# Output projection weights loaded as one 36,864-byte run per partition, and the attention output projected in one piece at the end

## The chip, the core and the metric

The kernel runs on one core of a Trainium2 chip. The core has a matrix engine (TensorE, PE in the profile), VectorE (DVE), ScalarE (ACT), GpSimd (POOL) and SyncE (SP). SP and ACT issue transfers to 16 DMA engines that the core's queues share. On-chip data lies in SBUF and in the accumulators' memory PSUM, both with 128 partitions. The metric is device time in microseconds for one execution; lower is better.

## The reference

One decode step (one token) for a batch of 4, with an attention block and a small MLP side by side on the same normalised input. Cut to what matters:

```python
xn = layernorm(A_x)                                   # [4, 1, 576]
# attention: 32 query heads, 16 key/value heads, the last W = 2048 positions of 8192
q  = (xn @ wq) as [4, 32, 1, 128]
s  = einsum("bhqd,bhkd->bhqk", q, k[:, :, -2048:]) * 128 ** -0.5
o  = einsum("bhqk,bhkd->bhqd", softmax(s), v[:, :, -2048:])
A  = o as [4, 1, 4096] @ wo                           # wo: [4096, 576]
# MLP: 576 -> 576 (gelu) -> 576, residual x1, 576 -> 4608 (gelu) -> 576
B  = x1 + gelu(layernorm(x1) @ w3) @ w4               # w4: [4608, 576]
out = A_x + A + B                                     # bf16, [4, 1, 576]
```

Everything is bf16 outside the accumulators. The caches that are read take 2 x 16 x 2 MB, wo 4.7 MB, wq 4.7 MB, w3 and w4 5.3 MB each.

## The kernel before

Instructions are recorded with a key by `add` and `add_dma`, sorted by key on each engine, and written out engine by engine, each with its semaphore waits (lines 163 to 176 and 543 to 603). An engine's own order is therefore fixed; the engines meet through semaphores. The two long stages are hardware loops of four iterations, one for the keys and one for the values.

**Transfers.** All loads but the 4-row input come from SP's queue, in this order: wq, w1, w2, w3, keys of the 16 key/value heads (2 MB each, ring `kring` of four slots), values (2 MB each, ring `vring` of four slots), with wo behind the fourth value load, and four pieces of w4 at the end (`W4P`: row tiles 0 to 14, 14 to 28, 28 to 34, 34 to 36 of 36). A key or value load puts 128 runs of 16,384 bytes on 128 partitions; its source is walked as 32 blocks of positions by 4 batches. Value load g waits until the product with the values of head g - 4 has been read (`PV{g-4}`), so value load 4 waits for `PV0`. wo waits for `T119`, since it overwrites the key ring. It is read as `(h p r) n -> p h (r n)`: partition p gets, for each of 8 groups of 512 rows, 4 neighbouring rows (4,608 bytes), which makes 1,024 runs. w4 piece n waits for the last value product that uses its part of `vring` (`PV12`, `PV13`, `PV14`, `PV14`).

**Keys.** PE transposes each 128x128 block of keys (line 332), DVE and ACT copy the result to SBUF (lines 339, 340), PE multiplies it with the queries (line 348). Softmax over all heads follows at once (lines 374 to 409).

**Values.** For each of the 16 heads g, `pe_PV` (line 416) runs 64 matmuls of 8 columns, and DVE multiplies the result by the reciprocal sums into eight columns of `OTn` (line 424). `OTn` is [128 features, 128 (head, batch) columns].

**Output projection.** `AO_CH` cuts the 16 heads in two chunks. `pe_sel` (line 434) brings `OTn`'s rows into wo's row order by 16 matmuls with columns of the identity, DVE copies that to `ORT` (line 458), and `pe_AO` (line 441, by `acc_mm`) multiplies with wo. Chunk 0 (48 matmuls) stands inside the value loop under a condition on the third iteration, behind `PV11`; chunk 1 (16 matmuls) stands behind the loop. The matmuls have 4 columns of weights and 288 moving columns. The 576 outputs are two halves in two 32-column tiles of the PE array, `ACC[0]` at partition 0 in PSUM bank 0 and `ACC[1]` at partition 32 in bank 1. The same two accumulators take x + x1 (`pe_t1`) and all of w4's products (`MO0`, `MO1`, `MO2`, and for the last piece `MOl0` and `MOl1`, one for each half). Two copies to SBUF (lines 539, 540) and two 4-row stores, from SP and from ACT, end the program.

Of the kernel before, what the change touches and what calls it, by code (L numbers as in the profile page):

```python
# [5 lines left out]
FP32 = mybir.dt.float32  # L6
BF16 = mybir.dt.bfloat16
ACTF = mybir.ActivationFunctionType
# [9 lines left out]
NIT = 4  # L18
ACT_EVAC = (1, 4, 7)
WO_AFTER = 3  # L20
V0_AFTER = 8
AO_CH = ((0, 6), (6, 8))
W4P = ((0, 14), (14, 28), (28, 34), (34, 36))


# [13 lines left out]
def bass_parallel_sum__sliding_block_cached__mixer_s_mlp__decode_kernel(  # L39
# [22 lines left out]
    with ExitStack() as ctx:  # L62
        def sb(name, shape, dt):
            return ctx.enter_context(nc.sbuf_tensor(name, shape, dt))
# [13 lines left out]
        w3rag = regB_t[:, 4 * F:W3E]  # L78
        wqmain = vring_t[:, 0:4 * Hq * Dh].rearrange("p (r n) -> p r n", r=4)
        wqrag = vring_t[:, 4 * Hq * Dh:4 * Hq * Dh + Hq * Dh // 2]  # L80
        wo_sb = kring_t[:, 0:Hq * D].rearrange("p (h r n) -> p h r n", h=8, r=4)
        _o = 4 * Hq * Dh + Hq * Dh // 2
        w1main = vring_t[:, _o:_o + 4 * D].rearrange("p (r n) -> p r n", r=4)
        _o += 4 * D
# [43 lines left out]
        PTs = sb("PTs", [128, NT, 32], BF16)  # L128
        PTg = sb("PTg", [128, NPG, NT, B, 2], BF16)
        OTn = sb("OTn", [128, 128], BF16)  # L130
        ORT = sb("ORT", [128, 4, 8, B], BF16)
        t1 = sb("t1", [B, D], FP32)
        out_t = sb("out_sb", [32 + B, HALF], BF16)
        out_sb = [out_t[32 * h:32 * h + B, :] for h in range(2)]

        ps = ctx.enter_context(nc.psum_tensor("ps", [128, 8, 512], FP32))[:]
        Sps = ps[:, 0:4, :]
        tb = [ps[:, 4 + k, :].bitcast(BF16).rearrange("p (t d) -> p t d", t=8) for k in range(NTB)]
        ACC = [ps[32 * k:32 * k + B, k, 0:HALF] for k in range(2)]
        ORps = ps[:, 2, 0:128].rearrange("p (r h b) -> p r h b", r=4, h=8)  # L140
        rinvps = ps[:, 3, 0:128]
        OTps = lambda g: ps[:, 4 + g % 4, 0:8]
        Qps = ps[:, 0:2, :]
# [19 lines left out]
        def add(engine, emit, waits=(), sig=None, key=0.0, loop=None):  # L163
            seqc[0] += 1
            prog[engine].append(Op(emit, waits, sig, key, seqc[0], loop))

        def add_dma(pairs, skey, waits=(), key=0.0, engine="sp"):
            if skey not in S:
                S[skey] = sem("s_" + "_".join(str(k) for k in (skey if isinstance(skey, tuple) else (skey,))))
            dma_count[skey] = dma_count.get(skey, 0) + 16 * len(pairs)  # L170

            def emit(e):
                for o_, i_ in pairs:
                    e.dma_start(o_, i_).then_inc(S[skey], 16)  # L174
            add(engine, emit, waits, None, key)
            return ("dma", skey, dma_count[skey])
# [57 lines left out]
        for g in range(G):  # L234
            kk = KS + g if g else V0_AFTER + 0.5
            w = [f"PV{g - NVS}"] if g >= NVS else (["hs1"] if g < WQ_SLOTS else [])
            ev_v.append(add_dma(kv_pairs(vring_t, g % NVS, A_v_cache, g), ("v", g % NVS), w, kk))
            if g == WO_AFTER:
                ev_wo = add_dma([(wo_sb.rearrange("p h r n -> p h (r n)"), A_wo.rearrange("(h p r) n -> p h (r n)", h=8, r=4))],
                                "wo", [wo_wait], kk + 0.1)  # L240
        w4_src = B_w4.rearrange("(p r) n -> p r n", r=RT)
        w4_sb = vring_t[:, 0:RT * D].rearrange("p (t n) -> p t n", n=D)
# [177 lines left out]
        for g in range(G):  # L420
            m = g % 4
            add("pe", pe_PV(g), waits=[("L", ("v", m), 16), ("L", ("pg", m), 1), ("L", ("on", m), 1)], sig=f"PV{g}", key=KV + g,
                loop=("v", g // 4))
            add("dve", lambda e, g=g: e.tensor_tensor(out=OTn[:, 8 * g:8 * g + 8], in0=OTps(g), in1=rinvB[:, 8 * g:8 * g + 8], op=ALU.mult),  # L424
                waits=["rinvB", f"PV{g}"], sig=("on", m), key=KV + g + 0.5)


        def pe_sel(a, z):
            def f(e):
                ov = OTn[:].rearrange("p (h q b e) -> p h q b e", h=8, q=2, b=B)  # L430
                ins = None
                for r in range(4):
                    for hh in range(4):
                        ins = e.matmul(ORps[32 * hh:32 * hh + 32, r, a:z, :], lhsT=ident_bf[:, r:128:4],
                                       rhs=ov[:, a:z, hh // 2, :, hh % 2], start=True, stop=True,
                                       tile_position=(0, 32 * hh), skip_group_check=True)
                return ins
            return f

        def acc_mm(e, h, lhsT, rhs, start=False, stop=False):  # L440
            return e.matmul(ACC[h], lhsT=lhsT, rhs=rhs, start=start, stop=stop, tile_position=(0, 32 * h))  # L441

        def pe_AO(a, z):
            def f(e):
                ins = None
                for hg in range(a, z):
                    for r in range(4):
                        for h in range(2):
                            ins = acc_mm(e, h, ORT[:, r, hg, :], wo_sb[:, hg, r, HALF * h:HALF * (h + 1)])
                return ins  # L450
            return f
        for n, (a, z) in enumerate(AO_CH):
            last = z == 8
            kk = KV + (20 if last else 2 * z - 0.4)
            lp = None if last else ("v", NIT - 2, "only")
            add("pe", pe_sel(a, z), waits=[("c", ("on", (2 * z - 1) % 4), (2 * z - 1) // 4 + 2)] + ([f"ORT{n - 1}"] if n else []),
                sig=f"sel{n}", key=kk, loop=lp)
            add("dve", lambda e, a=a, z=z: e.tensor_copy(out=ORT[:, :, a:z, :], in_=ORps[:, :, a:z, :]),  # L458
                waits=[f"sel{n}"], sig=f"ORT{n}", key=kk)
            add("pe", pe_AO(a, z), waits=[f"ORT{n}"] + ([ev_wo] if n == 0 else []), sig=f"AO{n}", key=kk + 0.1, loop=lp)  # L460

        def pe_t1(e):
            ins = None
# [59 lines left out]
        add("act", gelu2, waits=["h2_4"], sig="gelu2", key=KW + 0.1)  # L523
        add("dve", lambda e: e.transpose(h2T_sb[:].rearrange("p c i -> p (c i)"), PTb[:, 0:N2]), waits=["gelu2"], sig="h2T", key=KW + 0.2)  # L524

        last_p = len(W4P) - 1
        for n, (t0, t1_) in enumerate(W4P):
            def f(e, t0=t0, t1_=t1_, hs=(0, 1)):
                ins = None
                for t in range(t0, t1_):  # L530
                    for h in hs:
                        ins = acc_mm(e, h, h2T_sb[:, t, 0:B], w4_sb[:, t, HALF * h:HALF * (h + 1)], stop=(t == RT - 1))
                return ins
            if n < last_p:
                add("pe", f, waits=[ev_w4[n], "h2T"], sig=f"MO{n}", key=KT + 20 + n)
            else:
                for h in range(2):
                    add("pe", lambda e, f=f, h=h: f(e, hs=(h,)), waits=[ev_w4[n], "h2T"], sig=f"MOl{h}", key=KT + 20 + n + 0.1 * h)
# [21 lines left out]
        def emit_op(eng_name, engine, op, waited, it=None):  # L560
            for w in op.waits:
                if w[0] == "L":
                    engine.wait_ge(S[w[1]], it * w[2] + w[2] if w[2] > 1 else it + 1)
                    continue
                s_, v_ = resolve(w)
                if waited.get(s_.num, 0) >= v_:
                    continue
                if it is None:
                    waited[s_.num] = v_
                engine.wait_ge(s_, v_)  # L570
            ins = op.emit(engine)
            if op.sig is not None:
                ins.then_inc(S[eng_name] if isinstance(op.sig, str) else S[op.sig], 1)

        def emit_program(eng_name, engine):
            waited = {}
            ops = prog[eng_name]
            k = 0
            while k < len(ops):
                op = ops[k]  # L580
                if op.loop is None:
                    emit_op(eng_name, engine, op, waited)
                    k += 1
                    continue
                name = op.loop[0]
                z = k
                while z < len(ops) and ops[z].loop is not None and ops[z].loop[0] == name:
                    z += 1
                group, k = ops[k:z], z
                shapes = [[o for o in group if o.loop[1] == it and len(o.loop) == 2] for it in range(NIT)]  # L590
                assert all([o.waits for o in sh] == [o.waits for o in shapes[0]] for sh in shapes)
                only = [o for o in group if len(o.loop) == 3]
                assert group[-2 * len(shapes[0]) - len(only):][len(shapes[0]):][:len(only)] == only
                with engine.Fori(0, NIT) as it:
                    for o in shapes[0]:
                        emit_op(eng_name, engine, o, waited, it)
                    if only:
                        with engine.If(it == only[0].loop[1]):
                            for o in only:
                                emit_op(eng_name, engine, o, waited, it)  # L600

        for name, eng in (("sp", nc.sync), ("pool", nc.gpsimd), ("dve", nc.vector), ("act", nc.scalar), ("pe", nc.tensor)):
            emit_program(name, eng)
# [28 lines left out]
```

## Time and profile before

| | |
|---|---|
| median of 3 runs | 215.7 us (215.67 to 217.24) |
| the profiled execution's own time | 215.64 us |
| its span, first to last instruction | 214.4 us |
| bytes moved | 88.63 MB, 413 GB/s over the span |
| busy: PE, weight loads, DVE, ACT, POOL | 67%, 51%, 39%, 28%, 5% |
| granted TensorE clock, mean | 0.785 of full |

Times in the views are microseconds from the span's start. A row of the groups gives the line, engine and operation, the tile written and the tile read, the count, then busy time and mean length of one, then the idle time of the engine before them and what ended it. A row of the timeline gives start, length, engine and line. A row of the stages gives the stretch, then busy time and count for PE, PE's weight loads, DVE, ACT and POOL, then the granted clock, the mean busy share of the 16 DMA engines, and the rate. The chain of waits goes back from the last instruction to what released it.

### The profile page before, as it was taken

The page shows a single profiled execution, that of the slowest core. Times are in us where ns is not written, and L with a number is a line of the kernel's source. Part 1 is how long each engine was busy: PE and PEld are TensorE (multiplying, and loading weights), DVE is VectorE, ACT ScalarE, POOL GpSimd, SP SyncE. Part 2 cuts the span into 40 slices and gives each one's busy share as a digit, 9 for nine tenths or more (in the row PEclk, how much of TensorE's full clock was granted, in tenths as well). Part 3 has the DMA queues.
Part 4 walks back from the last instruction along what each step waited for, and adds up shares of the span by engine and source line. Part 5 has one row for each costly group of instructions (what it writes and reads, how often), then busy time and mean ns, then how long its engine had stood idle before and what let it go on. Part 6 is the DMA issues. An engine that isn't in the chain of part 4 may idle for free.

```text
span 214.4 us, 5735 instructions
## 1 busy us (share of the span) xinstructions
PE 143.2 (67%) x2646; PEld 109.1 (51%) x2648; DVE 84.5 (39%) x162; ACT 59.1 (28%) x71; POOL 10.0 (5%) x34
## 2 busy tenths in 40 slices
PE   0368375999999993999999719813343443973655
PEld 0115223777788883788877604813343443463523
DVE  5502603666666663466666479411111112100000
ACT  2000302566555553365666653000000000000000
POOL 8101000000010000000000000000000000000000
PEclk9999755999999999699999985555555555585589
DMA  6999999999999999999999999999999999999992
GB/s 245 434 395 439 440 410 437 428 408 431 428 431 422 431 428 434 422 434 423 431 425 431 428 407 411 424 427 431 419 434 431 431 419 434 428 434 421 424 412 113
DMA packets 7697, 88.63 MB, mean 413 GB/s; under 512 B 764, under 2 KB 1032, under 8 KB 2824
## 3 DMA queue, kind: packets, MB, share of 16 engines
q1 hardware_dynamic: 7672, 88.50, 97.8%
q8 instruction: 7, 0.11, 0.2%
q14 instruction: 2, 0.02, 0.0%
q10 hardware_dynamic: 16, 0.01, 0.0%
HBM read 88.49 MB, written 0.00 MB: 413 GB/s over the span
## 4 chain that ended last, share of the span: by engine, by line
DMA 53%; PE 36%; DVE 4%; SPq 4%; issue 2%; ACT 0%
DMA vring<-in_A_v_cache_dram 25%; PE ps L332 23%; DMA kring<-in_A_k_cache_dram 21%; PE ps L348 7%; DMA vring<-in_B_w_dram 7%; PE ps L416 5%; SPq L174 4%; DVE PTb L382 1%; DVE rmax L374 1%; DVE regB L340 1%; PE ps L441 1%; DVE PTs L390 1%; PE ps L405 0%; ACT P_sb L379 0%; DVE out_sb L539 0%
## 5 line engine op out<-in xcount | busy, mean ns | idle before, releaser
L340 DVE COPY regB<-ps 128x1024 bf16<-128x1024 bf16 x80 | 52.3, 687 | 34.7 <-PE ps L332 32.9
L332 PEld LDWEIGHTS ps<-perm_k,kring 128*128 128x128 bf16 x1024 | 58.7, 99 | 12.6 <-issue 8.7
L332 PE MATMUL ps<-perm_k,kring 128*128 128x128 bf16 x1024 | 62.1, 222 | 4.2 <-DMA kring<-in_A_k_cache_dram 4.2
L339 ACT ACTIVATE regB<-ps 128x1024 bf16<-128x1024 bf16 x48 | 47.7, 1023 | 41.4 <-PE ps L332 41.4
L416 PE MATMUL ps<-PTg,vring 128*128 128x8 bf16 x1024 | 29.2, 168 | 33.3 <-DMA vring<-in_A_v_cache_dram 31.4
L416 PEld LDWEIGHTS ps<-PTg,vring 128*128 128x128 bf16 x1024 | 28.1, 103 | 34.5 <-DMA vring<-in_A_v_cache_dram 24.3
L424 DVE TENSOR_TENSOR OTn<-ps,rinvB 128x8 bf16<-128x8 f32 x16 | 2.7, 167 | 57.3 <-PE ps L416 57.2
L540 ACT ACTIVATE out_sb<-ps 4x288 bf16<-4x288 f32 x1 | 0.4, 402 | 81.2 <-PE ps L441 81.2
L348 PE MATMUL ps<-regB,Qs 128*32 128x512 bf16 x272 | 18.7, 395 | 4.6 <-issue 3.5
L348 PEld LDWEIGHTS ps<-regB,Qs 128*32 128x32 bf16 x272 | 6.6, 97 | 10.8 <-issue 6.2
L393 DVE TENSOR_TENSOR PTg<-PTs,bmask 128x512 bf16<-128x512 bf16 x16 | 10.7, 682 | 0.0
L370 POOL COPY Qs<-Qpad 128x128 bf16<-128x128 bf16 x16 | 4.6, 296 | 93.5 <-PE ps L348 81.4
L441 PE MATMUL ps<-kring,ORT 128*4 128x288 bf16 x64 | 7.7, 431 | 0.7 <-DVE ORT L458 0.7
L441 PE MATMUL ps<-vring,h2T_sb 128*4 128x288 bf16 x72 | 5.3, 299 | 2.8 <-DMA vring<-in_B_w_dram 2.8
L511 PE MATMUL ps<-regB,x1nT 128*32 128x432 bf16 (+1 forms) x60 | 5.4, 522 | 2.1 <-DMA regB<-in_B_w_dram 1.6
L274 PE MATMUL ps<-ident_bf,xn_bf 4*128 4x4 bf16 x8 | 0.5, 169 | 8.8 <-DVE ragsrc L267 8.8
L296 PE MATMUL ps<-vring,xnT 128*32 128x512 bf16 x40 | 4.6, 629 | 1.8 <-DMA vring<-in_A_wq_dram 1.8
L441 PEld LDWEIGHTS ps<-kring,ORT 128*4 128x4 bf16 x64 | 3.8, 121 | 3.9 <-DVE ORT L458 0.9
L441 PEld LDWEIGHTS ps<-vring,h2T_sb 128*4 128x4 bf16 x72 | 3.0, 87 | 5.3 <-DMA vring<-in_B_w_dram 4.0
L383 PE MATMUL ps<-PTb,perm_p 128*128 128x512 bf16 x3 | 1.8, 608 | 4.9 <-DVE PTb L382 4.8
L274 PEld LDWEIGHTS ps<-ident_bf,xn_bf 4*128 4x128 bf16 x8 | 0.4, 112 | 8.8 <-POOL ones_f L210 6.3
L524 DVE STREAM_TRANSPOSE h2T_sb<-PTb 128x1152 bf16<-128x1152 bf16 x1 | 1.4, 1378 | 8.4 <-ACT PTb L521 8.4
(88 smaller groups left out, 61.7 us busy)
## 6 DMA issues: line engine op xcount, KB each, us to landing
kring<-in_A_k_cache_dram SPq DMA_DIRECT2D x16, 2048.0 KB, 16.1
vring<-in_A_v_cache_dram SPq DMA_DIRECT2D x16, 2048.0 KB, 17.6
regB<-in_B_w_dram SPq DMA_DIRECT2D x2, 2304.0 KB, 21.3
kring<-in_A_wo_dram SPq DMA_DIRECT2D x1, 4608.0 KB, 24.1
vring<-in_A_wq_dram SPq DMA_DIRECT2D x2, 2048.0 KB, 9.5
vring<-in_B_w_dram SPq DMA_DIRECT2D x2, 2016.0 KB, 15.7
vring<-in_B_w_dram SPq DMA_DIRECT2D x2, 576.0 KB, 13.8
vring<-in_B_w_dram SPq DMA_DIRECT2D x1, 864.0 KB, 14.7
```

The costliest lines, as they stand in the source:

```text
L174: e.dma_start(o_, i_).then_inc(S[skey], 16)
L296: ins = e.matmul(Qps[32 * j:32 * j + 32, k, :], lhsT=x_, rhs=w, start=(r == 0), stop=(r == 4), tile_position=(0, 32 * j))
L332: ins = e.transpose(tb[n % NTB][:, t, :], kring[:, g % NKS, 8 * k + t, :], perm_k[:])
L339: return "act", lambda e: e.activation(out=ktbuf[:, n % NKT], in_=src, func=ACTF.Copy)
L340: return "dve", lambda e: e.tensor_copy(out=ktbuf[:, n % NKT], in_=src)
L348: ins = e.matmul(Sps[32 * b:32 * b + 32, c4, :].rearrange("p (t i) -> p t i", t=16), lhsT=Qs[:, g % 4, b, :], rhs=kttile[:, t0:t0 + 16, b, :],
L370: P(lambda e, g=g: e.tensor_copy(out=Qs[:, g % 4], in_=Qpad[:, g]), waits=(["qT"] if g == 0 else []) + ([f"SC{g - 4}"] if g >= 3 else []), ...
L393: add("dve", lambda e, g=g: e.tensor_tensor(out=PTg[:, g % NPG], in0=PTs[:, :, 2 * g:2 * g + 2].unsqueeze(2).to_broadcast([128, NT, B, 2]) ...
L416: ins = e.matmul(OTps(g), lhsT=vring[:, g % NVS, t, :], rhs=PTg[:, g % NPG, t].rearrange("p b e -> p (b e)"), start=(t == 0), stop=(t == N ...
L424: add("dve", lambda e, g=g: e.tensor_tensor(out=OTn[:, 8 * g:8 * g + 8], in0=OTps(g), in1=rinvB[:, 8 * g:8 * g + 8], op=ALU.mult), waits=[ ...
L441: return e.matmul(ACC[h], lhsT=lhsT, rhs=rhs, start=start, stop=stop, tile_position=(0, 32 * h))
L511: ins = e.matmul(H2ps[k][32 * j:32 * j + 32, :], lhsT=x_, rhs=w, start=(r == 0), stop=(r == 4), tile_position=(0, 32 * j))
```

## The change

Three things are done together.

wo is loaded as `(h q r) n -> q h (r n)` with 4 values of q, 32 heads h and 32 rows r: partition 32q + h gets one run of 32 neighbouring rows of head h, 36,864 bytes, which makes 128 runs. The source is walked with q outermost (4), then h (32).

The attention output is no longer brought into order by PE. DVE writes each head's result to strided columns of `OTn` (batch outermost), and once all 16 heads are done one DVE transpose of 32x32 blocks turns `OTn` into `ORT`. The condition in the value loop is gone, and all 64 matmuls with wo stand behind the loop.

These 64 matmuls, and those of w4's first piece (`FOLD` = 14 row tiles), go to four 32-column tiles in place of two. `ACC[2]` and `ACC[3]` lie at partitions 64 and 96 of PSUM bank 2. Behind `MO0` ACT copies both to SBUF as fp32 (`foldc`), and two fp32 matmuls with the identity add them to `ACC[0]` and `ACC[1]` (`fold`), ahead of `MO1`.

```diff
-AO_CH = ((0, 6), (6, 8))
+FOLD = 14
...
-        wo_sb = kring_t[:, 0:Hq * D].rearrange("p (h r n) -> p h r n", h=8, r=4)
+        wo_sb = kring_t[:, 0:32 * D].rearrange("p (r n) -> p r n", r=32)
...
+        fold_sb = P_sb[:, 0:2 * HALF].bitcast(FP32)
...
-        ACC = [ps[32 * k:32 * k + B, k, 0:HALF] for k in range(2)]
-        ORps = ps[:, 2, 0:128].rearrange("p (r h b) -> p r h b", r=4, h=8)
+        ACC = [ps[32 * k:32 * k + B, min(k, 2), 0:HALF] for k in range(4)]
...
-                ev_wo = add_dma([(wo_sb.rearrange("p h r n -> p h (r n)"), A_wo.rearrange("(h p r) n -> p h (r n)", h=8, r=4))],
+                ev_wo = add_dma([(kring_t[:, 0:32 * D], A_wo.rearrange("(h q r) n -> q h (r n)", q=4, r=32))],
...
-            add("dve", lambda e, g=g: e.tensor_tensor(out=OTn[:, 8 * g:8 * g + 8], in0=OTps(g), in1=rinvB[:, 8 * g:8 * g + 8], op=ALU.mult),
+            add("dve", lambda e, g=g: e.tensor_tensor(
+                out=OTn[:].rearrange("p (b g e) -> p g b e", b=B, e=2)[:, g], in0=OTps(g).rearrange("p (b e) -> p b e", b=B),
+                in1=rinvB[:, 8 * g:8 * g + 8].rearrange("p (b e) -> p b e", b=B), op=ALU.mult),
...
-        def pe_sel(a, z):
...
+        def acc_mm(e, h, lhsT, rhs, start=False, stop=False, k0=0):
+            return e.matmul(ACC[h], lhsT=lhsT, rhs=rhs, start=start, stop=stop, tile_position=(k0, 32 * h))
+
+        def pe_AO(e):
+            ins = None
+            for r in range(32):
+                for h in range(2):
+                    ins = acc_mm(e, 2 * (r % 2) + h, ORT[:, r:128:32], wo_sb[:, r, HALF * h:HALF * (h + 1)], start=(r == 1))
+            return ins
+        add("dve", lambda e: e.transpose(ORT[:], OTn[:]), waits=[("c", ("on", m), NIT + 1) for m in range(4)], sig="ORT", key=KV + 20)
+        add("pe", pe_AO, waits=["ORT", ev_wo], sig="AO", key=KV + 20)
...
+        def pe_fold(e):
+            ins = None
+            for h in range(2):
+                k0 = 64 + 32 * h
+                ins = acc_mm(e, h, ident_f[k0:k0 + B, k0:k0 + B], fold_sb[k0:k0 + B, :], k0=k0)
+            return ins
...
+        add("act", lambda e: e.activation(out=fold_sb[64:96 + B, :], in_=ps[64:96 + B, 2, 0:HALF], func=ACTF.Copy),
+            waits=[f"MO{n_fold}"], sig="foldc", key=KT + 20 + n_fold + 0.5)
+        add("pe", pe_fold, waits=["foldc"], sig="fold", key=KT + 20 + n_fold + 0.5)
...
-                        ins = acc_mm(e, h, h2T_sb[:, t, 0:B], w4_sb[:, t, HALF * h:HALF * (h + 1)], stop=(t == RT - 1))
+                        a = 2 * (t % 2) + h if t < FOLD else h
+                        ins = acc_mm(e, a, h2T_sb[:, t, 0:B], w4_sb[:, t, HALF * h:HALF * (h + 1)], stop=(t == RT - 1 or (t == FOLD - 1 and a > 1)))
```

PE's own order from the value loop to the end, before (row L416 is one pass through the loop's body, `ps` are accumulators in PSUM, `kring` holds wo by then and `vring` w4):

```order
L416 MATMUL ps<-PTg,vring 128x8 x256
L598 COMPARE_AND_BRANCH
L434 MATMUL ps<-OTn,ident_bf 32x24 x16
L441 MATMUL ps<-kring,ORT 4x288 x48
L598 UNCONDITIONAL_BRANCH
L594 REGISTER_ALU
L594 COMPARE_AND_BRANCH
L434 MATMUL ps<-OTn,ident_bf 32x8 x16
L441 MATMUL ps<-kring,ORT 4x288 x16
L441 MATMUL ps<-vring,h2T_sb 4x288 x72
```

The same place on PE with the change, where `P_sb` holds the two accumulators that are folded in:

```order
L416 MATMUL ps<-PTg,vring 128x8 x256
L584 REGISTER_ALU
L584 COMPARE_AND_BRANCH
L431 MATMUL ps<-kring,ORT 4x288 x64
L431 MATMUL ps<-vring,h2T_sb 4x288 x28
L431 MATMUL ps<-P_sb,ident_f 4x288 x2
L431 MATMUL ps<-vring,h2T_sb 4x288 x44
```

The 48 matmuls with wo have moved from inside the loop to behind it, the 32 matmuls of `pe_sel` are gone, and the fold stands between the first 28 and the other 44 matmuls with w4.

SP's queue around the load of wo, as a difference (the sizes are those of the destination; `kring` is wo's place):

```order
 L174 DMA kring<-in_A_k_cache_dram 128x1x8192 x7
 L174 DMA vring<-in_A_v_cache_dram 128x1x8192 x3
-L174 DMA kring<-in_A_wo_dram 128x8x2304
+L174 DMA kring<-in_A_wo_dram 128x1x18432
 L174 DMA vring<-in_A_v_cache_dram 128x1x8192 x12
 L174 DMA vring<-in_B_w_dram 128x8064 x2
```

The load of wo keeps its place, ahead of 12 value loads and w4; its destination has one run of 18,432 elements for each partition in place of eight of 2,304.

More of the change, by code (lines that the diff above doesn't have):

```diff
@@ L130, in bass_parallel_sum__sliding_block_cached__mixer_s_mlp__decode_kernel @@
         OTn = sb("OTn", [128, 128], BF16)
-        ORT = sb("ORT", [128, 4, 8, B], BF16)
+        ORT = sb("ORT", [128, 128], BF16)
         t1 = sb("t1", [B, D], FP32)
+        fold_sb = P_sb[:, 0:2 * HALF].bitcast(FP32)
         out_t = sb("out_sb", [32 + B, HALF], BF16)
@@ L423, in bass_parallel_sum__sliding_block_cached__mixer_s_mlp__decode_kernel @@
                 loop=("v", g // 4))
-            add("dve", lambda e, g=g: e.tensor_tensor(out=OTn[:, 8 * g:8 * g + 8], in0=OTps(g), in1=rinvB[:, 8 * g:8 * g + 8], op=ALU.mult),
+            add("dve", lambda e, g=g: e.tensor_tensor(
+                out=OTn[:].rearrange("p (b g e) -> p g b e", b=B, e=2)[:, g], in0=OTps(g).rearrange("p (b e) -> p b e", b=B),
+                in1=rinvB[:, 8 * g:8 * g + 8].rearrange("p (b e) -> p b e", b=B), op=ALU.mult),
                 waits=["rinvB", f"PV{g}"], sig=("on", m), key=KV + g + 0.5)
-        def pe_sel(a, z):
[L429 to L460, printed above, removed]
+        def acc_mm(e, h, lhsT, rhs, start=False, stop=False, k0=0):
+            return e.matmul(ACC[h], lhsT=lhsT, rhs=rhs, start=start, stop=stop, tile_position=(k0, 32 * h))
@@ L524, in bass_parallel_sum__sliding_block_cached__mixer_s_mlp__decode_kernel @@
         add("dve", lambda e: e.transpose(h2T_sb[:].rearrange("p c i -> p (c i)"), PTb[:, 0:N2]), waits=["gelu2"], sig="h2T", key=KW + 0.2)
+        def pe_fold(e):
[4 more added lines that the diff above has]
+            return ins
+        n_fold = [z for _, z in W4P].index(FOLD)
+        assert FOLD % 2 == 0
+        add("act", lambda e: e.activation(out=fold_sb[64:96 + B, :], in_=ps[64:96 + B, 2, 0:HALF], func=ACTF.Copy),
+            waits=[f"MO{n_fold}"], sig="foldc", key=KT + 20 + n_fold + 0.5)
+        add("pe", pe_fold, waits=["foldc"], sig="fold", key=KT + 20 + n_fold + 0.5)
         last_p = len(W4P) - 1
@@ L589, in emit_program @@
                 group, k = ops[k:z], z
-                shapes = [[o for o in group if o.loop[1] == it and len(o.loop) == 2] for it in range(NIT)]
+                shapes = [[o for o in group if o.loop[1] == it] for it in range(NIT)]
                 assert all([o.waits for o in sh] == [o.waits for o in shapes[0]] for sh in shapes)
-                only = [o for o in group if len(o.loop) == 3]
-                assert group[-2 * len(shapes[0]) - len(only):][len(shapes[0]):][:len(only)] == only
                 with engine.Fori(0, NIT) as it:
@@ L596, in emit_program @@
                         emit_op(eng_name, engine, o, waited, it)
[L597 to L600, printed above, removed]
         for name, eng in (("sp", nc.sync), ("pool", nc.gpsimd), ("dve", nc.vector), ("act", nc.scalar), ("pe", nc.tensor)):
```

## The prediction

> **What bounds the kernel now.** I read the page's transfer rows first, then the chain of waits, then the stages, and the timeline only at wo's transfer and at the end. The page's rows on the 16 DMA engines (busy tenths and rate in 40 slices of 5.36 us, then the queue's total) and its chain by engine:
>
> ```profile
> DMA  6999999999999999999999999999999999999992
> GB/s 245 434 395 439 440 410 437 428 408 431 428 431 422 431 428 434 422 434 423 431 425 431 428 407 411 424 427 431 419 434 431 431 419 434 428 434 421 424 412 113
> q1 hardware_dynamic: 7672, 88.50, 97.8%
> DMA 53%; PE 36%; DVE 4%; SPq 4%; issue 2%; ACT 0%
> ```
>
> The DMA engines are full from the first slice to the last. The end of the chain (start, length, what) shows no engine in their place:
>
> ```profile
> 157.37 17.64 DMA vring<-in_A_v_cache_dram
> 175.01 0.05 issue
> 175.06 1.89 PE ps L416 x64
> 176.94 0.02 issue
> 176.96 17.62 DMA vring<-in_A_v_cache_dram
> ...
> 196.53 14.69 DMA vring<-in_B_w_dram
> 211.22 0.04 issue
> 211.26 1.20 PE ps L441 x16
> 212.46 0.43 DVE out_sb L539
> ```
>
> Values arrive, PE takes 1.9 us for each head and waits again; 1.6 us of work follow w4's last bytes. So the time is bytes on the busiest DMA engine over its rate, plus a short tail. The stages give the rate (last three columns: granted clock, DMA share, GB/s):
>
> ```profile
> 20.00:118.00 98.00, 83.75 (x1300) 65.60 (x1303) 54.59 (x88) 48.42 (x53) 3.85 (x13) 0.91 1.01 427
> 126.00:139.00 13.00, 9.71 (x235) 7.15 (x237) 9.66 (x22) 3.98 (x10) 0.00 (x0) 0.52 1.01 408
> 145.00:205.00 60.00, 30.95 (x870) 25.77 (x872) 7.14 (x22) 0.00 (x0) 0.00 (x0) 0.53 1.01 428
> ...
> 208.00:209.00 1.00, 0.00 (x0) 0.00 (x0) 0.00 (x0) 0.00 (x0) 0.00 (x0) 1.00 0.85 353
> 209.00:210.00 1.00, 0.83 (x14) 0.62 (x16) 0.00 (x0) 0.00 (x0) 0.00 (x0) 1.00 0.92 369
> 210.00:211.00 1.00, 1.00 (x18) 0.53 (x12) 0.00 (x0) 0.00 (x0) 0.00 (x0) 1.00 0.47 189
> 211.00:212.00 1.00, 0.80 (x16) 0.50 (x16) 0.00 (x0) 0.00 (x0) 0.00 (x0) 1.00 0.13 51
> ```
>
> At 428 GB/s each of 16 engines moves 26.75 GB/s. Around wo's transfer (126 to 139) it is 408: the 4,608-byte runs cost something.
>
> **wo's load: how many engines carry it.** This term decides. The last two DMAs of the program are the two 4-row stores. The DMA view of 212.5 to the end holds nothing else:
>
> ```profile
> DMA packets 16, 0.00 MB, mean 2 GB/s; under 512 B 8, under 2 KB 16, under 8 KB 16
> q10 hardware_dynamic: 8, 0.00, 0.6%
> q1 hardware_dynamic: 8, 0.00, 0.5%
> ```
>
> Each store is 8 packets: 4 rows of 576 bytes and 4 under 512 B, which can only be the writes that report an engine done. The loads behave otherwise. q1's 7672 packets less the store's 8 are 7664; the 47 loads of SP's queue need 6912 runs (32 x 128 for keys and values, 1024 for wo, 14 x 128 for the other weights); the 752 left are 16 for each load. So a load of 128 rows reports from 16 engines, and a store whose walk has an outermost count of 4 from four. Key loads walk their source as 32 x 4 runs and still use 16, so an outermost count of 32 is enough. The new wo load walks its source as 4 x 32 runs: 4 outermost. By the nearest rows it goes to four engines. No row shows 128 destination partitions under an outermost 4; that is the open point, and the first rival.
>
> [...]
>
> On four engines each carries 32 x 36,864 = 1,179,648 bytes, against 64 x 4,608 = 294,912 before: 884,736 more, at 26.75 GB/s 33.1 us. Those four engines also carry their sixteenth of everything behind wo. SP's queue and what waits behind wo (start, length, DMAs issued; then K's and wo's median time from issue to landing):
>
> ```profile
> 116.69 0.39 SPq L174 DMA_DIRECT2D kring<-in_A_wo_dram  x1
> 134.27 23.64 SPq L174 DMA_DIRECT2D vring<-in_A_v_cache_dram  x7
> kring<-in_A_k_cache_dram SPq DMA_DIRECT2D x16, 2048.0 KB, 16.1
> kring<-in_A_wo_dram SPq DMA_DIRECT2D x1, 4608.0 KB, 24.1
> 145.92 1.85 PE L416 MATMUL ps<-PTg,vring 128*128 128x8 bf16 x64 [4.57 <-DMA vring<-in_A_v_cache_dram]
> ```
>
> SP issues value load 4 at 134.27, once `PV0` is done; its partitions lie on all 16 engines, so on four of them it queues behind wo, and its first matmul moves from 145.92 to about 179. wo lands about 24.1 + 33 = 57 us after its issue. Twelve engines finish loads 4 to 7 and then have nothing, since load 8 waits for `PV4`. They can't catch up, as the four need every us for their own bytes. So the 33.1 us are on the path whole.
>
> Bounds. Would an engine go faster with the others idle? At 210 to 211 us, with 0.47 of them busy, 189 GB/s is 189 / (0.47 x 16) = 25.1 GB/s for each: no. With that rate the term is 35.2. The best slice of the page, 440 GB/s, gives 27.5 and 32.2. I keep 26.75, the mean of the longest stages.
>
> [...]
>
> Two small gains. Longer runs: 13 us at 408 in place of 427 lost 13 x 19 / 427 = 0.6; 36,864-byte runs should win most of it, I take 0.5 (bounds 0 and 0.6). The ragged end: from 208 to 212 the shares add up to 0.85 + 0.92 + 0.47 + 0.13 = 2.37, so the mean engine ends at 210.4 and the last at about 211.26, where PE starts on its landing. Now four engines set the end, which may not be the late ones: 0.9 off as for mean engines (bounds 0 and 2.9, since some stop before 208.4).
>
> **The value loop.** PE and SP at the third iteration:
>
> ```profile
> 182.84 5.62 PE L441 MATMUL ps<-kring,ORT 128*4 128x288 bf16 x48 [0.45 <-DVE ORT L458]
> 190.19 7.14 SPq L174 DMA_DIRECT2D vring<-in_B_w_dram  x4
> 194.62 1.87 PE L416 MATMUL ps<-PTg,vring 128*128 128x8 bf16 x64 [2.85 <-DMA vring<-in_A_v_cache_dram]
> ```
>
> The 48 matmuls, their selection and copy leave the loop, some 6 us of PE. `PV12` and `PV13` come earlier by that, and w4's first issue too. It buys nothing: PE waits 2.85 us for values again at 194.62, and the queue still held two value loads at 190.19. The strided store of line 424 writes the same 8 elements behind work that waits on transfers.
>
> **The tail.** Relative to the landings it keeps its shape, since the four engines deliver values and w4 at the old pace. PE's rows before, and the rows that price what is new:
>
> ```profile
> 199.53 1.87 PE L416 MATMUL ps<-PTg,vring 128*128 128x8 bf16 x64 [3.03 <-DMA vring<-in_A_v_cache_dram]
> 202.25 2.08 PE L441 MATMUL ps<-kring,ORT 128*4 128x288 bf16 x16 [0.30 <-DVE ORT L458]
> 204.34 2.23 PE L441 MATMUL ps<-vring,h2T_sb 128*4 128x288 bf16 x28
> 209.17 1.88 PE L441 MATMUL ps<-vring,h2T_sb 128*4 128x288 bf16 x28 [2.60 <-DMA vring<-in_B_w_dram]
> ...
> 25.39 2.11 PE L511 MATMUL ps<-regB,x1nT 128*32 128x432 bf16 x24 [0.48 <-DVE x1nT L495]
> L382 DVE STREAM_TRANSPOSE PTb<-P_sb 128x512 bf16<-128x512 bf16 x4 | 2.7, 711 | 0.8 <-ACT P_sb L379 0.8
> L441 PE MATMUL ps<-t,ident_f 4*4 4x288 f32 x4 | 1.1, 656 | 0.0
> L540 ACT ACTIVATE out_sb<-ps 4x288 bf16<-4x288 f32 x1 | 0.4, 402 | 81.2 <-PE ps L441 81.2
> ```
>
> In before's times: the last product ends at 201.40, DVE scales it, and the new transpose of 128x128 is at most a 512-wide one (0.71), in proportion 0.2 to 0.3; PE starts on wo near 202.0. Line 511 runs on four column tiles: 24 matmuls of 384 columns on average in 2.11 us, 88 ns each, so 66 for 288 columns; 64 take 4.2 us, to 206.2. The two-tile rows are the other end: 130 ns (16 in 2.08), 8.3 us. `MO0`'s 28 took 2.23 on two tiles; four tiles and a rising clock make 1.2 (bounds 0.9 and 2.2), to 207.4. Then PE waits for `foldc` (0.4 and handing over) and folds (1.1, as `pe_t1`'s four passes): 209.0. Behind that wait stand `MO1`, `MO2` and the last pieces, which DVE, ACT and the stores await; but w4's second piece lands only at 209.17. So I count the tail at 0, with up to 0.8 if `MO0` keeps its old time.
>
> Sum: 33.1 - 0.5 - 0.9 + 0 = 31.7. Span 214.4 + 31.7 = 246.1; the profiled execution took 215.64, 1.24 more than its span, as the median of 215.7 does within 0.1. Forecast 247.3 us.
>
> **Rivals.**
> - *Sixteen engines all the same.* The split goes by the destination's 128 partitions, or by all runs. Then only the 0.6 us of longer runs are left: 215.1 us, no slower than before. For it: key loads have 4 batches as an inner count and 128 partitions, and fill 16 engines. Against it: their outermost count is 32, and where it is 4 the trace shows four. It decides if wo's issue to landing stays near 24 us. Chance 0.09.
> - *Four engines and a late tail.* If four tiles bring nothing over two, wo takes 8.3 us (to 210.3), `MO0` 2.2, the fold 1.6: 214.1 against 209.17, 4.9 late, of which `MO2`'s idle 0.2 is won back. 252.0 us. For it: 64 matmuls now stand where 16 stood. Against it: line 511's 88 ns. It decides from about 75 ns for a matmul with wo. Chance 0.11.
> - *Sixteen engines and a late tail.* 215.1 + 4.7 = 219.8 us. Chance 0.02.
> - *Fewer than four engines, or these four held up further*: over 253 us. Chance 0.03.
>
> **How the numbers follow.** The forecast has 0.75. Its range: 32.2 - 0.6 - 2.9 = 28.7 to 35.2 + 0.8 = 36.0 on 214.4 + 1.24, so 244.3 to 251.6; with the late tail's centre, 244 to 253. Left out are the first, third and last rival and part of the second's upper end, together near 0.2. Within 1% is what a measurement can't tell from no change: 0.08, nearly all of the first rival; faster by more 0.01; slower 0.91.
>
> **What would show it.** Right: wo 57 us from issue to landing; the DMA row down to 2 or 3 tenths and some 107 GB/s (4 x 26.75) for about 20 us before 179, when load 4's product starts; the last value product near 231; PE still waiting for w4's second piece. Wrong: a DMA row of nines throughout and a span near 214 (sixteen engines), or PE busy without a gap from the last value product to the end (late tail).

## The result: 294.4 us, 1.36 times as long

The changed kernel takes 294.44 us (median of 5 runs, 294.09 to 294.96), before 215.72 us. The ratio is 1.362, with a 95% interval of 1.357 to 1.367. The forecast was 247.3 us, range 244 to 253: the direction was right, and less than half of the loss was foreseen. The profiled execution's span is 293.4 us, 79.0 more than before.

The page of the changed kernel: DMA engines and rate in 40 slices of 7.3 us, the load queue, and the chain by engine.

```profile
DMA  7999999999999999958999982222222999999950
GB/s 287 410 440 416 434 429 423 424 429 429 429 427 431 426 429 429 429 209 177 202 197 211 189 152 69 55 60 65 60 84 107 355 384 429 431 433 421 428 221 24
q1 hardware_dynamic: 6764, 88.50, 81.0%
DMA 32%; another core or an unknown queue 29%; PE 28%; issue 4%; DVE 3%; SPq 3%; ACT 0%
```

The bytes are the same. Up to 125 us (the first 17 slices) nothing has changed. Then seven slices run at 152 to 211 GB/s, most of them with engines that are full nevertheless, seven more at 55 to 107 GB/s with a quarter of the engines busy, and from about 227 us the rate climbs back to the old one. The end of the chain of waits shows one hole:

```profile
144.32 0.94 PE ps L416 x30
145.26 78.85 another core or an unknown queue
224.34 1.85 PE ps L416 x64
226.19 2.79 another core or an unknown queue
...
256.01 17.63 DMA vring<-in_A_v_cache_dram
273.69 1.88 PE ps L416 x64
275.59 14.63 DMA vring<-in_B_w_dram
290.26 1.20 PE ps L431 x16
```

Value load 4's product starts at 224.34, before at 145.92: 78.4 us later, nearly the whole loss. Once the ring is full again the values come as before: a late value load stands in the chain with 17.63 us, before with 17.62. The unknown queue is most likely that of the value loads, a landing that the chain couldn't match: of the 119.8 us that PE idled ahead of line 416, the page puts 112.8 down to `vring`'s transfers.

The load queue's packets tell the engine count. Before it had 7672; 896 runs fewer (128 in place of 1024) make 6776, and 6764 are there: 12 reports are missing, so wo reported from 4 engines and not from 16.

The stages of the changed kernel, with the granted clock, the DMA share and GB/s at the end, show what those four did:

```profile
128.00:132.00 4.00, 3.89 (x45) 1.78 (x46) 3.93 (x9) 1.15 (x2) 0.00 (x0) 0.50 0.30 72
140.00:170.00 30.00, 0.94 (x30) 0.85 (x29) 0.77 (x2) 0.00 (x0) 0.00 (x0) 0.50 1.03 205
178.00:212.00 34.00, 0.00 (x0) 0.00 (x0) 0.00 (x0) 0.00 (x0) 0.00 (x0) 0.50 0.25 61
```

From 178 to 212 a quarter of the engines is busy, nothing else runs, and the four move 61 GB/s: 15 GB/s each, where the prediction had 26.75. From 140 to 170, with value loads 4 to 7 on the other twelve, all 16 are full and move 205 GB/s: half of before, for the value loads too.

### The profile page after: what moved, and what is told of

Same layout as the page of the kernel before. It is cut to its first block, busy times and chain, and to the rows that moved or that the text cites. A ratio compares the mean times of both kernels' runs of the same rounds, so it can differ in the third digit from the quotient of the medians.

```text
span 293.4 us, 5678 instructions
## 1 busy us (share of the span) xinstructions
PE 136.9 (47%) x2620; PEld 105.5 (36%) x2620; DVE 84.4 (29%) x161; ACT 59.7 (20%) x72; POOL 10.0 (3%) x34
## 3 DMA queue, kind: packets, MB, share of 16 engines
q1 hardware_dynamic: 6764, 88.50, 81.0%
## 4 chain that ended last, share of the span: by engine, by line
DMA 32%; another core or an unknown queue 29%; PE 28%; issue 4%; DVE 3%; SPq 3%; ACT 0%
PE ps L332 17%; DMA kring<-in_A_k_cache_dram 15%; DMA vring<-in_A_v_cache_dram 12%; PE ps L416 6%; PE ps L348 5%; DMA vring<-in_B_w_dram 5%; SPq L174 3%; DVE PTb L382 1%; DVE rmax L374 1%; DVE regB L340 0%; PE ps L431 0%; DVE PTs L390 0%; PE ps L405 0%; ACT P_sb L379 0%
## 5 line engine op out<-in xcount | busy, mean ns | idle before, releaser
L416 PE MATMUL ps<-PTg,vring 128*128 128x8 bf16 x1024 | 29.6, 168 | 119.8 <-DMA vring<-in_A_v_cache_dram 112.8
L416 PEld LDWEIGHTS ps<-PTg,vring 128*128 128x128 bf16 x1024 | 28.5, 104 | 121.0 <-issue 93.1
L332 PEld LDWEIGHTS ps<-perm_k,kring 128*128 128x128 bf16 x1024 | 58.0, 98 | 12.1 <-issue 8.6
L431 PE MATMUL ps<-vring,h2T_sb 128*4 128x288 bf16 x72 | 4.6, 326 | 0.7 <-DMA vring<-in_B_w_dram 0.7
L491 PEld LDWEIGHTS ps<-regB,x1nT 128*32 128x32 bf16 x60 | 2.2, 138 | 7.2 <-DMA regB<-in_B_w_dram 5.5
L504 DVE STREAM_TRANSPOSE h2T_sb<-PTb 128x1152 bf16<-128x1152 bf16 x1 | 1.4, 1378 | 10.9 <-ACT PTb L501 10.9
L383 PE MATMUL ps<-PTb,perm_p 128*128 128x512 bf16 x4 | 2.4, 610 | 4.3 <-DVE PTb L382 4.1
L431 PE MATMUL ps<-kring,ORT 128*4 128x288 bf16 x64 | 4.0, 444 | 0.7 <-DVE ORT L439 0.7
```

The source lines that it names most:

```text
L332: ins = e.transpose(tb[n % NTB][:, t, :], kring[:, g % NKS, 8 * k + t, :], perm_k[:])
L416: ins = e.matmul(OTps(g), lhsT=vring[:, g % NVS, t, :], rhs=PTg[:, g % NPG, t].rearrange("p b e -> p (b e)"), start=(t == 0), stop=(t == N ...
L491: ins = e.matmul(H2ps[k][32 * j:32 * j + 32, :], lhsT=x_, rhs=w, start=(r == 0), stop=(r == 4), tile_position=(0, 32 * j))
```

## The experiments

The records of single DMA packets in the trace give the time of one run or packet. They are used below:

```
kernel, packets                               one packet takes
before, wo 4,608 bytes (1024)                 0.182 us mean
before, values 16,384 bytes                   0.61 us median
changed, wo 36,864 bytes (128)                2.75 us mean (first 1.7, shortest 1.37, longest 4.23)
changed, values while wo is under way         1.25 us median or a little more
```

36,864 bytes in 1.37 us are 26.9 GB/s, an engine's old rate; 2.75 us are half of it. An engine carried 32 runs: 88 us, against 64 x 0.182 = 11.7 before. wo's last packet ends at 218.8, before at 140.3. Of the 88 us, 32 x 1.37 = 44 us belong to the four engines alone, which is the forecast's part, and the other 44 to the doubled time of a run.

Three theories could double it. P: the places that are written; two of the four engines write places where they get one engine's rate between them. L: a run of 36,864 bytes is slow in itself. M: the memory that is read holds up engines with such steps. All the variants below are of the changed kernel; a diff shows the place and the source of wo's load, not the whole call. The trace doesn't number the engines, so which engine writes which partitions is not shown; that engines split a load by its outermost count, in order, is an assumption. The runs without a ratio are one execution each; before's own times spread over some 1.5 us.

**The old load in the changed kernel.** It separates the load from all else.

```diff
-  [(kring_t[:, 0:32 * D], A_wo.rearrange("(h q r) n -> q h (r n)", q=4, r=32))]
+  [(kring_t[:, 0:32 * D].rearrange("p (c m) -> p c m", c=8), A_wo.rearrange("(c p r) n -> p c (r n)", c=8, r=4))]
```

> The changed kernel with wo loaded as before (1024 runs of 4,608 bytes, 16 engines); everything else of the change stays. wo's rows then don't match the order of the attention output, so the attention part of the result is wrong; the work and the waits are the same. If the whole loss is in the load, as all theories below say, the time is that of before or just under it: 214.5 to 216 us, with the 64 matmuls with wo in about 4 us on four column tiles and PE waiting for w4's second piece. If the later projection or the fold cost something too, it is 217 us or more.

Measured: 215.85 us against 215.83, ratio 0.9988 (0.9966 to 1.0011). The loss is in the load alone; four column tiles, the transpose and the fold neither cost nor bring anything that can be measured.

**Long runs on 16 engines.**

```diff
-  [(kring_t[:, 0:32 * D], A_wo.rearrange("(h q r) n -> q h (r n)", q=4, r=32))]
+  [(kring_t[:, 0:32 * D], A_wo.rearrange("(p r) n -> p (r n)", r=32))]
```

> wo in 128 runs of 36,864 bytes, but walked as 128 rows in one dimension, so 16 engines report. wo's rows don't match the attention output's order, so the attention part is wrong. In the changed kernel four engines moved wo at 61 GB/s together (178 to 212 us), 15 GB/s each, where 26.75 was assumed. [...] Theory L (a run of 36,864 bytes moves slowly in itself, 14 to 15 GB/s for each engine): 294,912 bytes per engine take 20 us in place of 11, about 224 us. [...]

Measured: 215.30 us, ratio 0.9971 (0.9948 to 0.9994). The queue's packets and the stage of wo's transfer in this run:

```profile
q1 hardware_dynamic: 6776, 88.50, 97.7%
126.00:139.00 13.00, 7.96 (x148) 4.79 (x149) 8.30 (x19) 3.98 (x10) 0.00 (x0) 0.51 1.01 434
```

6776 packets: the same 128 runs, with 16 reports. 434 GB/s where before had 408, 1.37 us for a run. Theory L is out, and the 0.5 us that the prediction gave to longer runs is there, once 16 engines move them (by the interval, 0.1 to 1.1 us).

**Four engines with another order of the destination.** Head 4i + j goes to partition 32q + 8j + i, so that each of the four, if they split the outermost count j, keeps to eight neighbouring partitions of each 32.

```diff
-  [(kring_t[:, 0:32 * D], A_wo.rearrange("(h q r) n -> q h (r n)", q=4, r=32))]
+  [(kring_t[32 * q:32 * q + 32, 0:32 * D], A_wo.rearrange("(i j q r) n -> q j i (r n)", i=8, j=4, q=4, r=32)[q]) for q in range(4)]
...
-  out=OTn[:].rearrange("p (b g e) -> p g b e", b=B, e=2)[:, g], ...
+  out=OTn[:].rearrange("p (b u e v) -> p u v b e", b=B, u=2, e=2, v=8)[:, g % 2, g // 2], ...
```

> wo in four loads of 32 partitions, each walked as 4 x 8 runs of 36,864 bytes (partition 32q + 8j + i holds head 4i + j, and the columns of the attention output are written in that order, so the result is the reference's). [...] Theory L: 36,864-byte runs stay slow, 290 to 296 us. Theory M: the steps through the source are other ones but four engines still read long strides, 280 to 296 us.

Measured: 267.67 us, below the 280 to 296 of L and M and above the prediction's 247.3. Three stages of it:

```profile
128.00:134.00 6.00, 5.76 (x72) 2.64 (x73) 5.93 (x12) 2.38 (x6) 0.00 (x0) 0.50 0.30 128
140.00:170.00 30.00, 0.94 (x30) 0.85 (x29) 0.77 (x2) 0.00 (x0) 0.00 (x0) 0.50 1.02 216
178.00:190.00 12.00, 0.00 (x0) 0.00 (x0) 0.00 (x0) 0.00 (x0) 0.00 (x0) 0.50 0.25 108
```

Alone (178 to 190) the four reach 108 GB/s, 27 each, 1.364 us for a run, where the changed kernel had 61 GB/s: another order of the destination ends the loss among the four. Beside values (140 to 170) everything is still halved (216 GB/s). So there are two losses: among the four, and between the four and the twelve. They also divide the 47 us by which the forecast was short: 26.8 are gone here (294.44 to 267.67), and 20.4 are left above 247.3. A run takes 1.98 us on average here, which for 32 runs is 20 us more than at 1.364.

**Short runs on the four engines.**

```diff
-  [(kring_t[:, 0:32 * D], A_wo.rearrange("(h q r) n -> q h (r n)", q=4, r=32))]
+  [(kring_t[:, 2304 * c:2304 * (c + 1)], A_wo.rearrange("(h q r) n -> q h (r n)", q=4, r=32)[:, :, 2304 * c:2304 * (c + 1)]) for c in range(8)]
```

> wo in eight loads, each walked as 4 x 32 runs of 4,608 bytes: four engines with the same partitions as in the changed kernel, but runs of the length that before had. The result is the reference's. [...] Theory L (long runs slow): each engine back at about 25 GB/s, 247 to 252 us. Theory M: about 294 us.

Measured: 260.66 us, above L's 247 to 252 and far below M's 294, which is also what the same partitions would give by P. SP's queue around the load of wo, then the four alone, then beside values:

```profile
116.78 36.17 SPq L174 DMA_DIRECT2D kring<-in_A_wo_dram  x8
153.00 60.00 SPq L174 DMA_DIRECT2D vring<-in_A_v_cache_dram  x9
130.00:155.00 25.00, 9.38 (x264) 7.65 (x263) 7.39 (x19) 0.60 (x2) 0.00 (x0) 0.50 0.26 106
161.00:180.00 19.00, 0.00 (x0) 0.00 (x0) 0.00 (x0) 0.00 (x0) 0.00 (x0) 0.50 1.01 235
```

The eight issues keep SP's queue busy until 152.95, so value load 4 is issued only at 153.00, and its packets come from 159 on: about seven tenths of wo move with nothing beside them. Alone the four reach 106 GB/s on the same partitions as in the changed kernel: 0.18 us for a short run, no loss among them. Beside values the rate is halved again, 0.33 us for a run.

P doesn't explain the first of these: the partitions are those of the changed kernel. Nor do the starts explain it: the four begin wo at 127.16, 127.27, 127.83 and 128.13, and in the changed kernel the starts are spread alike (127.08 to 128.28), which there is less than one long run. In the changed kernel, once the values are through, one engine's last runs take 1.67, 1.78, 2.73, 2.73, 1.67, 1.65, 2.73 and 2.75 us, a pattern that repeats every four runs. Why short runs on the same partitions go unslowed stays open.

**Sixteen engines, two partitions each of every 32.**

```diff
-  [(kring_t[:, 0:32 * D], A_wo.rearrange("(h q r) n -> q h (r n)", q=4, r=32))]
+  [(kring_t[32 * q:32 * q + 32, 0:32 * D], A_wo.rearrange("(h q r) n -> q h (r n)", q=4, r=32)[q]) for q in range(4)]
```

> wo in the change's own order (the result is the reference's), but as four loads of 32 partitions, one for each q, each walked as 32 rows in one dimension: 16 engines, two partitions each. [...] The two runs before this one have ruled out that long runs are slow (128 of them on 16 engines: 215.3 us) and shown four engines at full rate where they don't write neighbouring places at the same time (36,864 bytes in 1.36 us, against 2.73 in the changed kernel). [...] Theory M (the read side holds up four engines): 215 to 216 us.

Measured: 228.95 us, with 2.83 us for a run. wo's stage:

```profile
130.00:150.00 20.00, 8.54 (x233) 6.82 (x233) 6.42 (x16) 0.60 (x1) 0.00 (x0) 0.50 0.97 200
```

All 16 engines at half rate, eight runs each: 22.7 us in place of 11. M had 215 to 216. If each two share one engine's rate, as P has it, eight runs take 1.37 us more each, 11 us on before's 215.75: 226.7, an estimate, 2.2 under the measured time.

**Another source for the same destination.**

```diff
-  [(kring_t[:, 0:32 * D], A_wo.rearrange("(h q r) n -> q h (r n)", q=4, r=32))]
+  [(kring_t[:, 0:32 * D], A_k_cache[:, 0].rearrange("b s d -> b (s d)")[:, 0:1024 * D].rearrange("b (h m) -> b h m", h=32))]
```

> The changed kernel, with the load of wo reading another place: 4 x 32 runs of 36,864 bytes from the key cache, each of the four engines one unbroken stretch, the four 33.6 MB apart. The destination and the engines stay as in the changed kernel. wo's values are not loaded, so the attention part is wrong. Theory P: nothing changes, runs at 2.73 us where the four are alone, 290 to 296 us. Theory M (steps of 147,456 bytes in the source): runs at 1.37 us while alone, 250 to 270 us.

Measured: 294.90 us, and stage by stage the changed kernel again (205 and 61 GB/s there):

```profile
140.00:170.00 30.00, 0.94 (x30) 0.85 (x29) 0.77 (x2) 0.00 (x0) 0.00 (x0) 0.50 1.02 202
178.00:212.00 34.00, 0.00 (x0) 0.00 (x0) 0.00 (x0) 0.00 (x0) 0.00 (x0) 0.50 0.25 62
```

A quite different source changes nothing. Alone this would leave room for a second source that is slow too; but the next run reads wo in the changed kernel's own steps at 1.366 us a run. Theory M is out.

**A quarter of wo beside values, to partitions 0 to 15 and 32 to 47, and to 16 to 31 and 48 to 63.** The two differ in the destination only (`p0` is 0, then 16), and `WO_AFTER` is 5 in place of 3.

```diff
-  [(kring_t[:, 0:32 * D], A_wo.rearrange("(h q r) n -> q h (r n)", q=4, r=32))]
+  [(kring_t[p0 + 32 * c:p0 + 16 + 32 * c, 0:32 * D], A_wo.rearrange("(h q r) n -> q h (r n)", q=4, r=32)[:, 4 * c:4 * c + 4]) for c in range(2)]
```

> Only a quarter of wo, 32 runs of 36,864 bytes, walked as 4 x 4 runs twice, so on four engines with eight runs each (294,912 bytes an engine, as 16 engines would carry for all of wo), issued behind value load 5, so that the other 12 engines load values meanwhile. Three quarters of wo are not loaded, so the attention part is wrong. [...] The question is why in the changed kernel the value loads' 16,384-byte packets on the other engines took 1.25 us in place of 0.61 as long as wo was under way. [...] Theory M (reading wo beside values is slow): value packets near 1.25 us and wo's near 2.7 for the 11 to 22 us of wo, 222 to 228 us.

> [...] Theory M: as the run before.

Measured: 223.10 and 232.77 us. First partitions 0 to 15 and 32 to 47, a stage without and one with wo's transfer:

```profile
127.00:134.00 7.00, 5.78 (x71) 2.67 (x72) 6.72 (x13) 3.38 (x10) 0.00 (x0) 0.50 0.07 28
147.00:155.00 8.00, 1.87 (x64) 1.78 (x64) 0.77 (x2) 0.00 (x0) 0.00 (x0) 0.50 1.01 432
```

Then partitions 16 to 31 and 48 to 63, the stage with wo's transfer:

```profile
147.00:163.00 16.00, 1.87 (x64) 1.78 (x64) 0.76 (x2) 0.00 (x0) 0.00 (x0) 0.50 0.99 206
```

To the first partitions the four run wo at 1.366 us a run, the twelve run values at 0.61 us a packet, 432 GB/s together. To partitions 16 further on wo takes 2.73 us and values 1.25, 206 GB/s together. The destination is all that differs, so it is what halves the rate. And it halves it for all: each of the 16,384-byte packets that start between 146 and 164 takes 1.23 to 1.31 us, so all twelve engines are held up. How they come to be held up no run here shows. The 9.7 us between the two kernels are near the 10.9 that eight doubled runs make.

The 223.1 lie in M's 222 to 228, but at none of M's rates: they are 7.4 above before's 215.75 for a reason of their own. With wo two places further back the queue has nothing from 127 to 134 (0.07 of the engines busy), until `PV0` frees a slot for value load 4. wo's place in the queue covers that gap in before; by the share of idle engines (0.93 of 7 us) that is worth some 6.5 us, an estimate.

**A version that keeps the long runs.**

```diff
-  [(kring_t[:, 0:32 * D], A_wo.rearrange("(h q r) n -> q h (r n)", q=4, r=32))]
+  [(kring_t[:, 0:32 * D], A_wo.rearrange("(p r) n -> p (r n)", r=32))]
...
+  add("pe", lambda e: e.matmul(rinvps, lhsT=perm_p[:], rhs=ORT[:], start=True, stop=True), waits=["ORT"], sig="permO", key=KV + 20)
+  add("dve", lambda e: e.tensor_copy(out=ORTp[:], in_=rinvps), waits=["permO"], sig="ORTp", key=KV + 20)
-  add("pe", pe_AO, waits=["ORT", ev_wo], sig="AO", key=KV + 20)
+  add("pe", pe_AO, waits=["ORTp", ev_wo], sig="AO", key=KV + 20)
```

In `pe_AO` the weights are taken from `ORTp` in place of `ORT`.

> A version that keeps what the change was for and avoids what cost it: wo in 128 runs of 36,864 bytes walked as 128 rows in one dimension, so 16 engines each write their own partitions, and partition 4h + q gets rows 32q to 32q + 31 of head h. The transposed attention output, which has those at partition 32q + h, is brought to that order by one matmul with the permutation perm_p (already there for the softmax) and one DVE copy. Long runs alone gave 215.3 us against 215.83 (ratio 0.9971). The matmul and the copy add 0.5 to 0.7 us ahead of the products with wo; with PE's wait for w4's second piece that slack was 0.46 us in the changed kernel. So 215.2 to 215.7 us, ratio 0.996 to 1.000, and the attention part right. If the 0.5 us of long runs came from something else than the transfer of wo, 215.8.

Measured: 215.31 us against 215.81, ratio 0.9961 (0.9942 to 0.9979): 0.5 us faster than before, which is less than half a percent, and far faster than the change. Its tail on the timeline:

```profile
201.33 0.31 DVE L440 STREAM_TRANSPOSE ORT<-OTn 128x128 bf16<-128x128 bf16 x1
201.70 0.29 PE L441 MATMUL ps<-ORT,perm_p 128*128 128x128 bf16 x1 [0.71 <-DVE ORT L440]
202.03 0.29 DVE L442 CAST ORTp<-ps 128x128 bf16<-128x128 f32 x1 [0.38 <-PE ps L441]
202.37 4.01 PE L432 MATMUL ps<-kring,ORTp 128*4 128x288 bf16 x64 [0.38 <-DVE ORTp L442]
206.17 1.66 PE L432 MATMUL ps<-vring,h2T_sb 128*4 128x288 bf16 x28
208.34 0.65 PE L432 MATMUL ps<-P_sb,ident_f 4*4 4x288 f32 x4 [0.51 <-ACT P_sb L517]
```

The matmul and the copy put the products with wo 0.6 us later than in the run with long runs on 16 engines (202.37 against 201.76), and the fold still ends near 209. There the second piece of w4 had PE waiting until 208.83, so nothing is lost.

## Why the prediction was wrong, by its own steps

**What bounds the kernel**: right. The loss is a DMA engine's bytes over its rate, and nothing but the load of wo (0.9988 with the old load).

**How many engines carry wo**: right, from the two stores' 4 reports and the loads' 16. The changed kernel's 6764 packets show 4, and the first and the third rival fall with it.

**The four engines' rate**: this step failed. "884,736 more, at 26.75 GB/s 33.1 us", with bounds of 32.2 and 35.2. Measured: 36,864 bytes in 2.75 us on average, 13.4 GB/s, and wo's last packet 78.5 us later than before. The bounds asked only whether an engine gets faster or slower when others are idle. Two costs stood in the sum at nothing, without a reason: what the four do to each other (26.8 us, gone with another order of the destination) and what they and the value loads do to each other (some 20 us). Every row that the rate came from is of loads that go at 25 to 27.5 GB/s an engine; none has the rows split over the engines in another way, so none could price either cost, and the upper bound should have been open. The fourth rival, four engines "held up further", had 0.03 and came. That the destination sets both costs is shown (the two quarters, and the four engines with a different order); how it does so is not shown, and the short runs, unslowed while alone (106 GB/s), are not explained.

**"Twelve engines finish loads 4 to 7"**: they did, but at half their rate, near 176 us. The twelve's own delay cost nothing, since the four ended later still; what cost the some 20 us is that the four were slowed beside them.

**The landmarks**: wo was to land 57 us after its issue and took about 104 (115.33 to its last packet at 218.8). The DMA row fell to 2 tenths as forecast, but at about 60 GB/s, not 107, and for over 40 us, not 20. The last value product was to stand near 231 and stands at 273.69.

**Longer runs and the ragged end**: the gain of 0.5 was right on 16 engines (0.53 us at the median) and lost in the changed kernel; the 0.9 of the ragged end can't be told apart in it.

**The tail**: right that it adds nothing, with some luck in its parts. In the changed kernel:

```profile
281.15 4.02 PE L431 MATMUL ps<-kring,ORT 128*4 128x288 bf16 x64 [0.70 <-DVE ORT L439]
284.95 1.59 PE L431 MATMUL ps<-vring,h2T_sb 128*4 128x288 bf16 x28
287.05 0.65 PE L431 MATMUL ps<-P_sb,ident_f 4*4 4x288 f32 x4 [0.51 <-ACT P_sb L514]
288.16 1.88 PE L431 MATMUL ps<-vring,h2T_sb 128*4 128x288 bf16 x28 [0.46 <-DMA vring<-in_B_w_dram]
```

64 products in 4.02 us (forecast 4.2 from line 511's four tiles), the first piece of w4 in 1.59 (1.2), the fold in 0.65 (1.1), and PE still waits 0.46 us for w4's second piece. The first piece's 0.4 us too much and the fold's 0.45 too little cancel. The late tail, the second rival, did not come.

**The value loop**: right. With its 48 matmuls gone and the old load the time is that of before.

## What to carry to other kernels

Read a load's access pattern as the engines get it, outermost count first, and then ask which partitions will be written together, by this load and by the others under way. Longer runs were worth 0.5 us where the transfer was at 408 of 434 GB/s already; the split over four engines that hold each other up cost 79. The rate taken from rows where all engines go at full speed gave 33.1 us for the new split of the rows: here a lower bound of the time, not a middle.

## What the runs showed of the hardware that was not expected

The rate of a load depended on which partitions its engines wrote; two quite different sources gave the same times (294.4 and 294.9 us). Sixteen engines with two partitions each of every 32 took 2.83 us for 36,864 bytes, against 1.37 with 128 rows in one dimension; four engines alone went at 61 or 108 GB/s by the order of the destination. Worse, four engines that wrote partitions 16 to 31 and 48 to 63 beside value loads, in place of 0 to 15 and 32 to 47, halved all sixteen, from 432 to 206 GB/s; no run shows how. And four engines with runs of 4,608 bytes went at full rate while alone (106 GB/s) on the partitions where runs of 36,864 bytes reached 61 GB/s; that is not explained.
